# Fused attention and two dense blocks on one core: gate jobs spread through the second half, their stores on ScalarE's queue, and two moves in the attention phase

## The chip, the cores and the metric

The kernel runs on one core of one Trainium2 chip. The metric is the device time of one execution in microseconds (us). The engines go by the profile's names: PE (TensorE's matmuls) and PEld (its weight loads), DVE (VectorE), ACT (ScalarE), POOL (GpSimd) and SP (SyncE, which here only issues DMAs).

## The reference

Three blocks follow each other, on 4 batches of 448 rows and 768 columns (12 heads of 64).

```
attn = sigmoid(q @ k.T / sqrt(64) - log(448)) @ v        # per batch and head
x    = attn, heads side by side                           # 4 x 448 x 768

h    = (x.T @ U @ V).T                                    # mixes the rows, rank 32
u    = x + h
y    = u + relu(u @ w_ch1) @ w_ch2                        # 768 -> 3072 -> 768

gate = sigmoid(sum over k of conv_w[k] * y[row - 4 + k])  # 5 taps along the rows
out  = (gate * (y @ w_val)) @ w_out
```

## The kernel before, in words

**Products.** Every matmul operand is kept as a high and a low half, and `mm3` multiplies three times: high by high, high by low, low by high. The third of the three is thus the first to read the low half of its weights:

```
mm(ps, wk[:, 0], x[:, 0], start=start, stop=False, **kw)    # L438
mm(ps, wk[:, 0], x[:, 1], start=False, stop=False, **kw)    # L439
mm(ps, wk[:, 1], x[:, 0], start=False, stop=stop, **kw)     # L440
```

The high half is a copy on ACT (`in_two`, L200), the low half a subtraction on DVE (L203) that `in_two` puts into the list `deferred`; `flush()` writes that list out at the next part of a product.

**Three phases.** The attention phase has 12 rounds of two (batch, head pair)s: `scores` (L523), sigmoid (L511), `values` (L554), and `scores_rest`, `attend_rest` (L567) for the last columns of both pairs, after which `attend_rest` copies both results to `xs` (L576). Between these stand slots `(round, 0)`, `(round, 1)`, `(round, 2)`, in which `between()` runs what the table `side` holds: units that mix the rows of a finished batch (`mix_units`; `add` multiplies `h` at L758 and adds it to `xs` at L761), and preparations of weights.

The main phase computes y for two halves of the batches, first batches 0 and 1, then 2 and 3. A half has six quads q of four row blocks of the hidden layer. A quad has two chains, c = 0 and c = 2, of seven products each (`seven`), and then `ch2` four times, which multiplies the four relu'd blocks h by w_ch2 and adds the result to `xs` (L939). In a chain the products are `x` (A11), `y` (A12), `x` (S2), `z` (S1), `x` (S3), `z` (S4 with B22), and `x` (A22), which runs inside the next chain or ch2. The weights' combinations A and S are the work of DVE and ACT. Three copies on ACT (L807) save sums that the next product would write on: `p1`, `u2`, `p5`. `p5` copies z after S1; the part S4 writes z again, so its first matmul waits for that copy.

The last phase computes the gate of batches 2 and 3, the products with w_val and w_out, and the output.

**What decides the order of the side work.** `plan()` fills the list `jobs` in an order written by hand, and `step()`, which a product calls at its end, takes one job of it by `pump()`, at a few steps two. In the second half a quad has the jobs of the four row blocks' weights (`pair_jobs`, `second_jobs`), the preparation of w_val and w_out (`form_jobs`, the list `more`, for five of the six quads), and three jobs for one gate of batches 0 and 1 (`gate_jobs`): `first` (a scaled copy on ACT, L993, and one add on DVE, L989), `second` (two adds) and `third` (one add, then the sigmoid on ACT, L1005, then the store of 448 KB, L1010, on SP's queue). An add reads and writes 128 x 896 values. At the ends of the first three quads, `u_sums` also forms and parks sums T of y on DVE and ACT.

**Queues.** Every engine works its instructions in order, SP's DMA issues too. Loads of w_ch1's and w_ch2's prepared parts (L159, L417), of raw w_val (L163) and stores of prepared parts (L332) share SP's queue.

Of the kernel before, what the change touches and what calls it, by code (L numbers as in the profile page):

```python
# [30 lines left out]
NP = B * H // 2  # L31
# [16 lines left out]
def tile_kernel(  # L48
# [18 lines left out]
    nc = tc.nc  # L67
    mm = nc.tensor.matmul
    f32 = lambda ap: ap.bitcast(F32)
    deferred = []  # L70
# [4 lines left out]
    def flush(every=False):  # L75

        while deferred:
            now, deferred[:] = deferred[:], []
            for part in now:
                part()  # L80
            if not every:
                return
# [65 lines left out]
    gates_kept = {}  # L148
# [383 lines left out]
    def scores_rest(q):  # L532

        ps = pools["ps_s"].tile([P, 2, 512], F32, tag="sc", name=f"sl{q}")
        for j in range(2):
            kq, _ = raws.pop(2 * q + j)
            for h in range(2):
                r = slice(D * h, D * h + D)
                mm(
                    ps[D * j:D * j + D, h, :S],  # L540
                    kq[r, 0, NKC * SC + USED:],
                    kq[r, 1],
                    start=True,
                    stop=True,
                )
        rests[q] = rests[q], sigmoid(f"al{q}", ps)
# [15 lines left out]
    def attend_rest(q):  # L562
        vl, a = rests.pop(q)
        for j in range(2):
            r = slice(D * j, D * j + D)
            for h in range(2):
                mm(  # L567
                    pairs[2 * q + j][2]["ps"][D * h:D * h + D, :S],
                    vl[r, h],
                    a[r, h],  # L570
                    start=False,
                    stop=True,
                )
        for j in range(2):
            b, m = divmod(2 * q + j, KC)
            nc.vector.tensor_copy(x_of(b, m), pairs.pop(2 * q + j)[2]["ps"][:, :S])  # L576
# [404 lines left out]
    def gate_jobs(bs, m):  # L981

        t = []
        r = slice(bs[0], bs[-1] + 1)
        y = lambda k: xs[:, m, r, k:k + S]
        tap = lambda k: f32(cw[:, m * TAPS + k:m * TAPS + k + 1])

        def add(k):
            nc.vector.scalar_tensor_tensor(t[0], y(k), tap(k), t[0], op0=ALU.mult, op1=ALU.add)  # L989

        def first():
            t.append(operand(f"g{bs[0]}_{m}", F32)[:, :, :])
            nc.scalar.activation(t[0], y(0), AF.Copy, scale=tap(0))  # L993
            deferred.append(lambda: add(1))

        def second():
            add(2)
            add(3)

        def third():  # L1000
            add(4)
            deferred.append(sigmoid)

        def sigmoid():
            nc.scalar.activation(t[0], t[0], AF.Sigmoid)  # L1005
            deferred.append(put)

        def put():
            gates_kept[m] = pools["gates"].tile([P, 2, S], F32, tag="gates", name=f"gk{m}")
            nc.sync.dma_start(gates_kept[m][:, :, :], t[0])  # L1010

        return [(0, first), (0, second), (0, third)]

# [17 lines left out]
    def attention_phase():  # L1031


        for p, kq in enumerate([load_kq(p) for p in range(2)]):
            load_v(p, kq)
        nc.vector.memset(bias, -math.log(S))
        warm = scratch("warm")[:, :1]
        nc.scalar.activation(warm, bias, AF.Sigmoid)
        nc.gpsimd.memset(xs[:, :, :, :PAD], 0.0)

        zeros = operand("zeros")
        nc.vector.memset(f32(zeros[:, 0]), 0.0)
        idle = pools["ps_s"].tile([P, 2, 512], F32, tag="sc", name="idle")
        for _ in range(IDLE):
            mm(idle[:, 0, :S], zeros[:, 0, :P], zeros[:, 0], start=True, stop=True)
        prep_pair(0)
        load_pair(2)
        consts = load_mix()
        steps = prep_mix(*consts)
        side = {(0, 2): steps[:1], (1, 1): steps[1:2], (1, 2): steps[2:]}  # L1050
        for b in halves[0]:
            units = mix_units(b)
            r = 3 * b + 3
            for at, some in (
                ((r, 2), units[:2]),
                ((r + 1, 0), units[2:4]),
                ((r + 1, 2), units[4:5]),
                ((r + 2, 0), units[5:6]),
                ((r + 3, 0) if b == 0 else (r + 2, 2), units[6:]),
            ):  # L1060
                side[at] = some
        rounds = NP // 2
        todo = [part for k in range(KH) for part in u_sums(0, k)]
        def put(at, *parts):
            side[at] = side.get(at, []) + list(parts)

        put((0, 2), *[lambda: load_next(nc.sync)] * RAWS)
        at = iter([(q, k) for q in range(1, rounds) for k in range(3)][2:])
        for key in full_keys + part_keys:
            for part in ahead[key]:  # L1070
                slot = next(at)
                side[slot] = [part] + side.get(slot, [])
        for slot, n in (((9, 0), 1), ((9, 1), 1), ((9, 2), 2), ((10, 0), 1), ((10, 1), 1), ((10, 2), 2), ((11, 0), 1)):
            put(slot, *todo[:n])
            del todo[:n]
        for slot, n in (((10, 1), 1), ((10, 2), 1), ((11, 0), 1), ((11, 1), 2), ((11, 2), 2)):
            put(slot, *[pump] * n)

        def values(p):
            for c in range(NKC):  # L1080
                attend(p, c)

        def between(q, k):
            for step in side.get((q, k), ()):
                step()

        for q in range(rounds):
            p = 2 * q
            for c in range(NKC):
                scores(p, c)  # L1090
            flush()
            last = q == rounds - 1
            if q:
                values(p - 1)
                if last:
                    attend_rest(q - 1)
                between(q, 0)
                if not last:
                    attend_rest(q - 1)
            else:  # L1100
                prep_pair(1)
            if not last:
                scores_rest(q)
            flush()
            load_pair(p + 3)
            load_pair(p + 4)
            between(q, 1)
            prep_pair(p + 2)
            for c in range(NKC):
                scores(p + 1, c)  # L1110
            flush()
            values(p)
            between(q, 2)
            prep_pair(p + 3)
        scores_rest(rounds - 1)
        flush()
        pump()
        flush()
        values(NP - 1)
        attend_rest(rounds - 1)  # L1120

    full_keys = [("w2", n, half) for half in range(2) for n in range(QUAD)]
    part_keys = [("w2", n, 0) for n in range(QUAD, 2 * QUAD)]
# [2 lines left out]
    def plan():  # L1126

        for key in full_keys + part_keys:
            ahead[key] = ahead_jobs(*key, key in full_keys)
        def give(items):  # L1130
            for n, job, key in items:
                if key:
                    loads.append(key)
                jobs.append((n, job))

        rest = []
        for q in range(NQ):
            c1, c2 = (pair_jobs(0, QUAD * q + c) for c in (0, 2))
            w = second_jobs(0, q) if q else ready_jobs(0)
            w0, w1 = w[:len(w) - QUAD], w[len(w) - QUAD:]  # L1140
            raw, made = c2[:2] + c2[3:5], c2[2:3] + c2[5:]
            if not q:
                c1 = c1[:2] + c1[3:5] + c1[2:3] + c1[5:]
            a = c1[:4] + rest[:1] + c1[4:6] + rest[1:] + c1[6:7]
            for x in zip(raw, c1[7:] + [None]):
                a += x
            give(x for x in a if x)
            w01 = w0 + w1[:2]
            b = []
            for i in range(max(len(made), len(w01))):  # L1150
                b += made[i:i + 1] + w01[i:i + 1]
            if not q:
                b = made + w01
            give(b)
            rest = w1[2:]
        give(rest)
        more = [job for kind in ("val", "out") for k in range(KH) for job in form_jobs(kind, k)]
        share = -(-len(more) // (NQ - 1))
        for q in range(NQ):
            give(pair_jobs(1, QUAD * q))  # L1160
            a = pair_jobs(1, QUAD * q + 2) + (second_jobs(1, q) if q else ready_jobs(1))
            rest = [(*job, None) for job in gate_jobs(halves[0], q)] + more[:share]
            n = len(a)
            for i, job in enumerate(a):
                give([job] + rest[i * len(rest) // n:(i + 1) * len(rest) // n])
            del more[:share]
# [288 lines left out]
```

## Time and profile before

| | |
|---|---|
| three runs | 1014.51, 1015.64, 1016.39 us; median 1015.64 |
| the profiled execution | 1018.02 us; its span 1016.2 us |
| PE busy | 995.3 us (98%) |
| PEld busy | 843.1 us (83%) |
| DVE busy | 734.3 us (72%) |
| ACT busy | 464.3 us (46%) |
| mean granted TensorE clock | 0.993 of full speed |

The span reaches from the first instruction to the last; what the execution took beyond it, 1.8 us, lies around it. Times in rows count from the span's start. The attention phase lasts until about 150 us, the second half of the main phase from about 475 to 835 us.

### The profile page before, as it was taken

Reading aid. Unit: us, or ns where it says so; the run is one execution under the profiler, and the core shown is the slowest. Engines: PE = TensorE matmul, PEld = TensorE weight load, DVE = VectorE, ACT = ScalarE, POOL = GpSimd, SP = SyncE. Lnnn points to the kernel's source line nnn. Section 1 sums busy time; section 2 is a strip of 40 time slices with the busy share of each in tenths; the row PEclk is TensorE's granted clock in tenths of the full one; section 3 lists DMA queues with packets and bytes.
Section 4 is the critical chain, followed back from the end, with each engine's and each line's share of the span. In section 5 each row is a group of like instructions: output and inputs, shape, how many; then the busy total and the mean of one; then the engine's idle time right before and its main releaser. Section 6 shows DMA issues by size and latency. Waiting matters only on the chain.

```text
span 1016.2 us, 14576 instructions
## 1 busy us (share of the span) xinstructions
PE 995.3 (98%) x5208; PEld 843.1 (83%) x5208; DVE 734.3 (72%) x1324; ACT 464.3 (46%) x871; POOL 21.1 (2%) x39
## 2 busy tenths in 40 slices
PE   9999999999999999999989899998999999999998
PEld 5554448988888999999978798997999999999997
DVE  4767797658587888889466888878787667993631
ACT  6766685344352545546243453535353433431321
POOL 0111110000000000000000000000000000000000
PEclk9999999999999999999999999999999999999999
DMA  7967656625366686767274573735545186833845
GB/s 187 270 190 203 162 147 187 193 80 163 96 161 188 189 251 188 220 204 266 105 236 156 197 251 137 244 117 205 181 136 190 55 319 199 283 125 114 258 144 185
DMA packets 83048, 187.51 MB, mean 185 GB/s; under 512 B 15008, under 2 KB 34704, under 8 KB 82976
## 3 DMA queue, kind: packets, MB, share of 16 engines
q1 hardware_dynamic: 79840, 174.64, 55.0%
q0 software_dynamic: 2832, 11.60, 3.9%
q8 instruction: 41, 0.67, 0.3%
q10 hardware_dynamic: 304, 0.34, 0.1%
q14 instruction: 31, 0.25, 0.1%
HBM read 129.14 MB, written 57.41 MB: 184 GB/s over the span
## 4 chain that ended last, share of the span: by engine, by line
PE 91%; DVE 5%; DMA 2%; ACT 1%; issue 1%; SPq 0%; DVEq 0%; ACTq 0%
PE ch L438 11%; PE ch L439 11%; PE ch L440 11%; PE x L438 5%; PE x L440 5%; PE x L439 5%; PE av L554 5%; PE sc L523 5%; PE z L438 3%; PE z L440 3%; PE z L439 3%; PE x_fin L438 1%; PE x_fin L440 1%; PE val L439 1%; PE val L438 1%; PE x_fin L439 1%
## 5 line engine op out<-in xcount | busy, mean ns | idle before, releaser
L438 PE MATMUL ch<-h,w 128*128 128x448 f32 x576 | 212.8, 369 | 4.0 <-DMA w<-s_w 4.0
L439 PE MATMUL ch<-h,w 128*128 128x448 f32 x576 | 211.6, 367 | 0.0
L440 PE MATMUL ch<-h,w 128*128 128x448 f32 x576 | 211.5, 367 | 0.0
L939 DVE TENSOR_TENSOR xs<-ch,xs 128x1344 f32<-128x1344 f32 x48 | 74.6, 1555 | 68.0 <-PE ch L440 67.7
L438 PEld LDWEIGHTS ch<-h,w 128*128 128x128 f32 x576 | 108.5, 188 | 16.3 <-issue 4.3
L440 PEld LDWEIGHTS ch<-h,w 128*128 128x128 f32 x576 | 108.5, 188 | 9.7
L439 PEld LDWEIGHTS ch<-h,w 128*128 128x128 f32 x576 | 108.6, 189 | 9.5
L511 ACT ACTIVATE a<-sc,bias 128x896 f32<-128x896 f32 x72 | 67.6, 1010 | 11.0 <-PE sc L523 10.8
L104 DVE SCALAR_TENSOR_TENSOR x_w<-x_w,r_w 128x384 uint32<-128x384 uint32 x84 | 46.9, 559 | 29.8 <-ACT x_w L100 23.6
L554 PE MATMUL av<-a,vr 128*64 128x448 f32 x288 | 59.4, 548 | 0.0
L523 PEld LDWEIGHTS sc<-ks 64*128 64x128 f32 x432 | 38.8, 190 | 22.6 <-issue 6.6
L523 PE MATMUL sc<-ks 64*128 64x448 f32 x432 | 53.9, 389 | 1.9 <-DVE ks L500 0.8
L100 ACT ACTIVATE x_w<-raw_w 128x384 f32<-128x384 f32 x84 | 45.6, 546 | 19.9 <-DMA raw_w<-in_w 6.3
L440 PE MATMUL x<-T,S 128*128 128x448 f32 x144 | 52.9, 367 | 0.0
L438 PE MATMUL x<-T,S 128*128 128x448 f32 x144 | 52.8, 366 | 0.0
L439 PE MATMUL x<-T,S 128*128 128x448 f32 x144 | 52.7, 366 | 0.0
L554 PEld LDWEIGHTS av<-a,vr 128*64 128x64 f32 x288 | 18.5, 136 | 30.0 <-issue 26.7
L200 ACT ACTIVATE S<-raw_x_w 128x384 fp32r<-128x384 f32 x48 | 23.0, 517 | 37.2 <-PE ch L440 17.6
L200 ACT ACTIVATE A<-x_w 128x384 fp32r<-128x384 f32 x36 | 18.5, 522 | 46.3 <-PE ch L440 40.8
L200 ACT ACTIVATE A<-raw_x_w 128x384 fp32r<-128x384 f32 x36 | 18.2, 519 | 40.4 <-PE ch L440 37.1
L438 PE MATMUL z<-B,S 128*128 128x448 f32 x72 | 27.5, 382 | 7.8 <-ACT p L807 7.8
L807 ACT ACTIVATE p<-x 128x448 f32<-128x448 f32 x24 | 13.1, 545 | 47.7 <-PE x L440 45.0
(303 smaller groups left out, 2188.3 us busy)
## 6 DMA issues: line engine op xcount, KB each, us to landing
raw_w<-in_w SPq DMA_DIRECT2D x79, 384.0 KB, 3.8
kq<-in_kq SPq DMA_DIRECT2D x46, 224.0 KB, 4.4
raw_x_w<-k_w SPq DMA_DIRECT2D x24, 384.0 KB, 3.6
k_w<-x_w SPq DMA_DIRECT2D x43, 192.0 KB, 4.0
f_val_A<-s_val_A SPq DMA_DIRECT2D x21, 384.0 KB, 3.8
f_out_S<-s_out_S SPq DMA_DIRECT2D x20, 384.0 KB, 3.5
k_h<-x_w SPq DMA_DIRECT2D x36, 192.0 KB, 3.7
raw_w<-in_w POOLq DMA_DIRECT2D x17, 384.0 KB, 4.5
```

The costliest lines, as they stand in the source:

```text
L100: nc.scalar.activation(f32(x), f32(high), AF.Prelu, scale=2.0 ** -112, alpha=-(2.0 ** 32))
L104: nc.vector.scalar_tensor_tensor(x, x, 3, r, op0=ALU.logical_shift_left, op1=ALU.bitwise_or)
L200: nc.scalar.activation(t[:, 0], x, AF.Copy)
L438: mm(ps, wk[:, 0], x[:, 0], start=start, stop=False, **kw)
L439: mm(ps, wk[:, 0], x[:, 1], start=False, stop=False, **kw)
L440: mm(ps, wk[:, 1], x[:, 0], start=False, stop=stop, **kw)
L511: nc.scalar.activation(a[:, :, :], ps[:, :, :S], AF.Sigmoid, bias=bias, scale=1.0 / math.sqrt(D))
L523: mm(ps[:, h, :S].rearrange("p (c s) -> p c s", c=NSC), ks[r, tk, 0, c], ks[r, tq, 1, :, :SC], start=t == 0, stop=t == 2,)
L554: mm(att["ps"][D * h:D * h + D, :S], vr[:, h, c], a[:, h], start=c == 0, stop=False,)
L807: nc.scalar.activation(t, ps, AF.Copy)
L939: nc.vector.tensor_add(y, three[:, :, :S], y)
```

## The change

Four things are edited.

- A finished gate is stored by ACT's DMA queue right behind the sigmoid, in the same step; before, `put` was deferred and issued by SP.
- `plan()` puts the three gate jobs among the form jobs of the quad (at one sixth, one half and five sixths of them) and no longer ahead of them. In the last quad there are no form jobs and nothing changes.
- In the attention phase the last mix unit of batch 1 goes from slot (8, 2) to (9, 0), one place later. Batch 0's stood one place later already.
- In the last round, `scores_rest` comes ahead of the jobs of slot (11, 2), and `values` and `attend_rest` come ahead of the last `pump()`.

```
         def sigmoid():
             nc.scalar.activation(t[0], t[0], AF.Sigmoid)
-            deferred.append(put)
-
-        def put():
             gates_kept[m] = pools["gates"].tile([P, 2, S], F32, tag="gates", name=f"gk{m}")
-            nc.sync.dma_start(gates_kept[m][:, :, :], t[0])
+            nc.scalar.dma_start(gates_kept[m][:, :, :], t[0])
...
-                ((r + 3, 0) if b == 0 else (r + 2, 2), units[6:]),
+                ((r + 3, 0), units[6:]),
...
             values(p)
+            if last:
+                scores_rest(q)
             between(q, 2)
             prep_pair(p + 3)
-        scores_rest(rounds - 1)
-        flush()
+        values(NP - 1)
+        attend_rest(rounds - 1)
         pump()
         flush()
-        values(NP - 1)
-        attend_rest(rounds - 1)
...
-            rest = [(*job, None) for job in gate_jobs(halves[0], q)] + more[:share]
+            rest = more[:share]
+            for i, job in enumerate(gate_jobs(halves[0], q)):
+                rest.insert((2 * i + 1) * len(more[:share]) // 6 + i, (*job, None))
```

**Place 1: the first chain of the second quad.** Names are tiles: `g_1` is the gate of column block 1, `p_1_4`, `x_4` and `z_4` belong to the chain of row blocks 4 and 5 in the second half, `T_y` are the sums that are parked. DVE before, around the three last adds of the gate:

```order
L989 SCALAR_TENSOR_TENSOR g_1_5796<-xs,cw,g_1_5796 128x896
L584 TENSOR_TENSOR T_y_5799<-T_T_y_5738,T_y_5799 128x448
L584 TENSOR_TENSOR T_y_5801<-T_T_y_5738,T_y_5801 128x448
L864 TENSOR_TENSOR p_1_4_5794<-p_1_4_5794,y_4_5798 128x448
L251 TENSOR_TENSOR raw_x_w_7_1_5742<-raw_x_w_7_1_5742 128x384
L252 TENSOR_TENSOR raw_x_w_6_1_5673<-raw_x_w_7_1_5742,raw_x_w_6_1_5673 128x384
L989 SCALAR_TENSOR_TENSOR g_1_5796<-xs,cw,g_1_5796 128x896 x3
L859 SCALAR_TENSOR_TENSOR h_2_5836<-p_1_4_5794,h_2_5836 128x448
L256 TENSOR_TENSOR raw_x_w_6_1_5673<-raw_x_w_6_1_5673 128x384
L864 TENSOR_TENSOR p_1_4_5848<-p_1_4_5848,x_4_5774 128x448
```

The same stretch of DVE now:

```order
L584 TENSOR_TENSOR T_y_5797<-T_T_y_5738,T_y_5797 128x448
L584 TENSOR_TENSOR T_y_5799<-T_T_y_5738,T_y_5799 128x448
L864 TENSOR_TENSOR p_1_4_5794<-p_1_4_5794,y_4_5796 128x448
L203 TENSOR_TENSOR A_val_5810<-x_val_0_5652,A_val_5810 128x384
L203 TENSOR_TENSOR A_val_5812<-x_val_1_5668,A_val_5812 128x384
L251 TENSOR_TENSOR raw_x_w_7_1_5742<-raw_x_w_7_1_5742 128x384
L252 TENSOR_TENSOR raw_x_w_6_1_5673<-raw_x_w_7_1_5742,raw_x_w_6_1_5673 128x384
L101 TENSOR_SCALAR r_val_0_5841<-raw_val_0_5745 128x384
L104 SCALAR_TENSOR_TENSOR x_val_0_5840<-x_val_0_5840,r_val_0_5841 128x384
L859 SCALAR_TENSOR_TENSOR h_2_5847<-p_1_4_5794,h_2_5847 128x448
L989 SCALAR_TENSOR_TENSOR g_1_5860<-xs,cw,g_1_5860 128x896
L864 TENSOR_TENSOR p_1_4_5858<-p_1_4_5858,x_4_5774 128x448
```

Of the four adds one is left in this chain. On ACT the copy `p5` of z_4 (which is written to `p_1_4_5848`, and now to `p_1_4_5858`) stood behind the gate's sigmoid:

```order
L807 ACTIVATE u_1_4_5833<-x_4_5774 128x448
L858 ACTIVATE h_2_5836<-p_1_4_5794 128x448
L1005 ACTIVATE g_1_5796<-g_1_5796 128x896
L807 ACTIVATE p_1_4_5848<-z_4_5775 128x448
L200 ACTIVATE A_val_5864<-x_val_0_5652 128x384
```

It now stands behind a relu, with the gate's first copy behind it:

```order
L807 ACTIVATE u_1_4_5838<-x_4_5774 128x448
L100 ACTIVATE x_val_0_5840<-raw_val_0_5745 128x384
L858 ACTIVATE h_2_5847<-p_1_4_5794 128x448
L807 ACTIVATE p_1_4_5858<-z_4_5775 128x448
L993 ACTIVATE g_1_5860<-xs,cw 128x896
```

The sigmoid and the store behind it stand some thirty instructions later, among the splits that run beside ch2.

**Place 2: the end of the second chain of the same quad, ahead of ch2.** `w_1_4_0` is the first block of w_ch2 that ch2 reads, and its low half is the L203 row. DVE before:

```order
L203 TENSOR_TENSOR A_1_6_5973<-raw_x_w_7_1_5742,A_1_6_5973 128x384
L859 SCALAR_TENSOR_TENSOR h_2_5975<-p_1_6_5911,h_2_5975 128x448
L353 TENSOR_TENSOR x_val_1_5668<-x_val_1_5668,x_val_0_5652 128x384
L864 TENSOR_TENSOR p_1_6_5989<-p_1_6_5989,x_6_5894 128x448
L203 TENSOR_TENSOR w_1_4_0_6003<-raw_x_h__2_1_5918,w_1_4_0_6003 128x384
L203 TENSOR_TENSOR w_1_5_0_6004<-raw_x_h__2_1_5918,w_1_5_0_6004 128x384
```

And now:

```order
L353 TENSOR_TENSOR x_val_1_5668<-x_val_1_5668,x_val_0_5652 128x384
L989 SCALAR_TENSOR_TENSOR g_1_5860<-xs,cw,g_1_5860 128x896 x2
L859 SCALAR_TENSOR_TENSOR h_2_5967<-p_1_6_5913,h_2_5967 128x448
L203 TENSOR_TENSOR A_1_6_5984<-raw_x_w_7_1_5742,A_1_6_5984 128x384
L864 TENSOR_TENSOR p_1_6_5982<-p_1_6_5982,x_6_5897 128x448
L203 TENSOR_TENSOR S_val_5999<-x_val_0_5652,S_val_5999 128x384
L203 TENSOR_TENSOR S_val_6001<-x_val_0_5840,S_val_6001 128x384
L357 TENSOR_TENSOR x_val_0_5840<-x_val_1_5886,x_val_0_5652 128x384
L864 TENSOR_TENSOR u_1_6_5965<-u_1_6_5965,z_6_5898 128x448
L203 TENSOR_TENSOR w_1_4_0_6019<-raw_x_h__2_1_5891,w_1_4_0_6019 128x384
L203 TENSOR_TENSOR w_1_5_0_6020<-raw_x_h__2_1_5891,w_1_5_0_6020 128x384
```

The two adds of the gate are new in this chain. The two low halves of `S_val`, the sum L357 and the sum `u` with `z_6` stood behind the low half of `w_1_4_0` and now stand ahead of it. In the next three quads the two adds stand in the same chain too, a few rows ahead of the low half of the block that ch2 reads first, but `u` stays behind it.

**Place 3: SP's queue in the first quad of the second half.** `w_1_0_0` is again the first block that ch2 reads, here a load of a part prepared long before. Before:

```order
L1010 DMA gk_5345<-g_0_5285 128x896
L163 DMA raw_val_1_5364<-in_wval 128x384
L163 DMA raw_val_0_5391<-in_wval 128x384
L163 DMA raw_val_1_5409<-in_wval 128x384
L163 DMA raw_val_0_5417<-in_wval 128x384
L332 DMA s_val_A_5434<-A_val_5428 128x768
L332 DMA s_val_A_5437<-A_val_5430 128x768
L417 DMA w_1_0_0_5450<-s_w_0_0_446 128x768
```

And now:

```order
L332 DMA s_val_A_5377<-A_val_5367 128x768
L332 DMA s_val_A_5380<-A_val_5369 128x768
L163 DMA raw_val_1_5402<-in_wval 128x384
L163 DMA raw_val_0_5420<-in_wval 128x384
L163 DMA raw_val_1_5428<-in_wval 128x384
L159 DMA raw_x_w_4_1_5444<-k_w_2138 128x768
L417 DMA w_1_0_0_5458<-s_w_0_0_446 128x768
```

The two stores went from just ahead of the load to further up, a load of a part of w_ch1 (L159) came in just ahead of it, and the gate's store has left the queue.

## Rows read from the trace of the kernel before

**Rows 1.** The page: busy time by engine, and the chain that ended last.

```profile
PE 995.3 (98%) x5208; PEld 843.1 (83%) x5208; DVE 734.3 (72%) x1324; ACT 464.3 (46%) x871; POOL 21.1 (2%) x39
...
PE 91%; DVE 5%; DMA 2%; ACT 1%; issue 1%; SPq 0%; DVEq 0%; ACTq 0%
```

**Rows 2.** Waits of PE over the span: waiter, releaser, total us, times, longest.

```profile
PE z L438 <- ACT p L807: 7.8, 3, 3.1
PE ch L438 <- DMA w<-s_w: 4.0, 2, 3.0
...
PE y L438 <- DVE xs L576: 1.0, 1, 1.0
...
PE sc L523 <- DVE xs L761: 0.7, 1, 0.7
```

**Rows 3.** Timeline, PE, second quad: start, duration, line, tiles, [idle before, releaser].

```profile
568.96 0.36 PE L440 MATMUL x<-T,S 128*128 128x448 f32 x1
572.40 0.47 PE L438 MATMUL z<-B,S 128*128 128x448 f32 x1 [3.08 <-ACT p L807]
...
573.35 0.58 PE L439 MATMUL z<-B,S 128*128 128x448 f32 x1
573.72 0.58 PE L440 MATMUL z<-B,S 128*128 128x448 f32 x1
```

**Rows 4.** Timeline, DVE, the same stretch.

```profile
567.41 3.52 DVE L989 SCALAR_TENSOR_TENSOR g<-xs,cw,g 128x896 f32<-128x896 f32 x3
```

**Rows 5.** Timeline, ACT, the same stretch.

```profile
570.97 0.95 ACT L1005 ACTIVATE g<-g 128x896 f32<-128x896 f32 x1 [3.92 <-DVE g L989]
571.83 0.53 ACT L807 ACTIVATE p<-z 128x448 f32<-128x448 f32 x1
```

**Rows 6.** Busy us by engine in six stretches; last three: granted clock, DMA share, GB/s.

```profile
525.00:530.00 5.00, 4.01 (x13) 3.65 (x14) 0.00 (x0) 0.00 (x0) 0.00 (x0) 0.66 0.99 340
570.00:575.00 5.00, 2.60 (x9) 2.35 (x10) 4.29 (x8) 3.94 (x8) 0.00 (x0) 0.83 0.38 147
575.00:580.00 5.00, 5.00 (x23) 4.57 (x22) 3.00 (x8) 1.35 (x3) 0.00 (x0) 0.83 0.56 184
630.00:635.00 5.00, 4.13 (x13) 3.71 (x14) 3.35 (x8) 3.54 (x8) 0.00 (x0) 0.66 0.48 170
690.00:695.00 5.00, 3.72 (x13) 3.34 (x14) 3.67 (x8) 3.46 (x7) 0.00 (x0) 0.78 0.23 92
700.00:800.00 100.00, 100.00 (x486) 90.83 (x485) 74.64 (x130) 42.80 (x89) 0.00 (x0) 1.00 0.49 164
```

**Rows 7.** Timeline, SP's DMA issues, first quad of the second half.

```profile
519.93 0.80 SPq L332 DMA_DIRECT2D s_val_A<-A_val  x2
520.77 0.53 SPq L417 DMA_DIRECT2D w<-s_w  x1
```

**Rows 8.** Timeline, PE, the start of that quad's ch2.

```profile
522.59 0.37 PE L440 MATMUL z<-B,S 128*128 128x448 f32 x1
525.99 0.71 PE L438 MATMUL ch<-h,w 128*128 128x448 f32 x1 [3.03 <-DMA w<-s_w]
```

**Rows 9.** Timeline, DVE, second quad, the end of its second chain.

```profile
587.12 0.62 DVE L864 TENSOR_TENSOR p<-p,x 128x448 f32<-128x448 f32 x1 [0.86 <-ACT S_val L200]
587.65 1.02 DVE L203 TENSOR_TENSOR w<-raw_x_h__2_1_5918,w 128x384 fp32r<-128x384 f32 x2
```

**Rows 10.** Timeline, PE, second quad: the third matmul of its ch2.

```profile
589.08 0.36 PE L440 MATMUL ch<-h,w 128*128 128x448 f32 x1
```

**Rows 11.** Line L989, the gate's adds: count, duration in ns, first and last start.

```profile
L989 DVE SCALAR_TENSOR_TENSOR g<-xs,cw,g x24: 1142/1147/1153, 502.6 to 821.9; 128x896 f32<-128x896 f32 x24
```

**Rows 12.** Timeline, DVE, the end of the attention phase.

```profile
152.11 0.35 DVE L101 TENSOR_SCALAR r_w<-raw_w 128x384 uint32<-128x384 uint32 x1
...
153.04 1.15 DVE L576 COPY xs<-av 128x448 f32<-128x448 f32 x2
...
155.12 1.02 DVE L203 TENSOR_TENSOR S<-x_w,S 128x384 fp32r<-128x384 f32 x2
```

## The prediction

> **What bounds the kernel now.** I read the page first, for the engine that leaves no room: PE is busy 98% of the span and makes up 91% of the chain that ended last, DVE 5%, DMA 2%, ACT 1% [rows 1]. So time is gained where PE stands still, or where its clock is low, and nowhere else; a DVE instruction or a DMA more costs nothing until PE waits for it. Second come PE's waits, which list those places. The reader is to see four of interest [rows 2]: `z` waits 7.8 us in three places for the ACT copy L807, ch2 waits 4.0 us in two places for loads of w_ch2, `y` waits 1.0 us for the copies L576, and `sc` 0.7 us for the mix unit's add L761.
>
> Third, the timeline of one `z` wait tells whose delay it is. DVE works on three gate adds from 567.41 for 3.52 us [rows 4]. The gate's sigmoid on ACT waits 3.92 us for them and runs at 570.97, and behind it in ACT's order, at 571.83, comes the copy p5 that the next product needs [rows 5]. PE, done with its matmuls at 568.96, goes on at 572.40 [rows 3].
>
> Fourth, the granted clock by stretch. It reads 0.66 to 0.83 of full speed in the stretches that follow stalls of this size, and 1.00 from 700 to 800 us, where PE does not wait [rows 6]. Two stretches of 5 us at 0.83 lack 1.7 us of full clock, as one at 0.66 does. That fits 3.4 us at the lower of the two levels, 1.2 instead of 2.4 GHz. In such a time a matmul starts every 0.37 us (573.35 and 573.72) [rows 3], against 0.206 us at the full clock (486 matmuls in the 100 us from 700 on [rows 6]). 3.4 us hold 9.2 matmuls, which take 1.9 us at 0.206. So each drop costs about 1.5 us. Four such drops follow stalls: one after ch2's wait at 522.6 and three after the `z` waits. The waits of about 1 us (ch2's other one of 4.0 less 3.0, and that of `y` [rows 2]) show none; I take a stall over 2 us as the condition, which is an estimate from these cases.
>
> **The change part by part.** The sum is made against the profiled execution, 1018.02 us; the median of the runs is 1015.64, so I carry the difference over to the median.
>
> *Gates spread, first chain.* Of the four gate adds that stood in a quad's first chain or the jobs around it, one stays there in the second quad, behind the copy's inputs; the sigmoid goes to ch2, where ACT has splits but no p5 to do. The copy p5 then follows a relu, and z ended long before. So all three `z` waits should go: 7.8 us [rows 2] and three drops of 1.5 us, 12.3 us. If adds of the second chain delayed its p5 in the same way, a part would come back; on ACT nothing that waits for a gate now stands ahead of a p5, so I take all of it. Bound from below: only two of three go, 8.2 us.
>
> *SP's queue in the first quad.* The two stores that stood just ahead of the load w_1_0_0 were issued at 519.93 and the load at 520.77 [rows 7], and the load landed for 525.99, 3.03 us late [rows 8]. The stores now go earlier, since their splits do, and the gate's store has left the queue. In front of the load stands a load of w_ch1, whose buffer comes free with a split on ACT; from the rows around, I put the issue at about 519.1, 1.7 us earlier. The 16 DMA engines are busy in that stretch, with a share of 0.99 [rows 6], and the transfers that move out of the stretch (the gate's store was done earlier anyway) relieve it by one to two of 384 KB; at 340 GB/s one takes 1.2 us. So the load arrives 1.7 to 4 us sooner, against 3.03 wanted. I take a stall of 0.3 left. Then the drop behind it goes too: 2.7 + 1.5 = 4.2 us. Bounds: 0 and 4.5. The second load wait, 1.0 us, is behind stores that also go earlier: 0.8 (0 to 1).
>
> *The adds' new place.* Second and third add are one job, 2 x 1.15 us [rows 11], and it now stands in the second chain. Before, the low half of w_1_4_0 began at 587.65 and took about 0.55, half of the row's 1.02 for two [rows 9]; its first reader, the third matmul of ch2, ran at 589.08 [rows 10]: 0.9 us to spare, and DVE had idled 0.86 shortly before [rows 9]. Now 2.3 us of adds, and some 1.5 us of low halves and a sum (three at about 0.5), stand ahead of it: 3.8 - 0.9 - 0.86 = 2.0 us late at most by this difference. Walked through in the new order, from the sum with x_4 on, 27 instructions at their spacings give 15.5 us and one wait for a relu 1.3; the low half is then 1.6 us late. And since the sum `u` now stands ahead of it and waits for the last matmul of z_6, it is late by about 0.9 even with an empty DVE. I take 1.6 for the second quad (0.9 to 2.0, with a drop 3.5). The same walk gives 0.55, 0 and 0.6 in the three quads after it, where `u` is not ahead and DVE has no more to do than before the adds: 2.7 in all, with 0.9 and 8 as ends. The first quad's low halves are loaded, so nothing there, and the last quad is unchanged.
>
> *The stores on ACT.* Six DMA issues come to ACT, in ch2 stretches where ACT is busy two fifths of the time (42.80 of 100 us [rows 6]) and PE reads nothing that is fresh from it. At the 0.5 us of an issue on SP (0.53 [rows 7]), six are 3 us in 100s of idle ones: 0. If ch2's splits waited for them, 3.
>
> *The two moves in attention.* The add L761 goes behind another product, and `sc` no longer waits for it: 0.7 (0 to 0.7). The copies L576 at 153.04 stood behind the unpacking that the last `pump()` gave DVE (from 152.11 on [rows 12]); they now run 0.9 earlier and `y` starts 0.9 earlier. But the next part needs the low half of S, whose row is at 155.12 [rows 12] and stays there, with the unpacking now behind the copies. So most is given back one product later: 0.25 (0.2 to 0.9).
>
> Sum: -12.3 - 4.2 - 0.8 + 2.7 + 0 - 0.7 - 0.25 = -15.55. 1018.02 becomes 1002.5, and the median 1015.64 becomes **1000.1; I say 1000**.
>
> **The rivals.** *The loads land no earlier.* What speaks for it: a DMA share of 0.99 when the load is under way [rows 6], so bytes, and not the issue, may set the landing. Then 4.2 and 0.8 stay: -10.55, 1005. Against it: the stores ahead of it are 768 KB, and they go earlier by more than their own transfer takes. The Trainium skill, "DMA: Bandwidth & Descriptors", section "Issuing engines are not separate DMA queues", says that DMAs started by different engines run on the same 16 DMA engines and interleave, so that another issuing engine saves issue time only; by that rule the gate's store leaves SP's queue without relief to the others, which is this rival's case. My sum rests on the times of issue, not on the store's new queue.
>
> *The adds' new place costs more.* The low half is late by over 2 us in two of the four quads and the clock falls each time: 2 x (2.0 + 1.5) + 1.2 = 8.2 instead of 2.7, -10, 1005.6; in all four 14, -4.3, 1011. For it: DVE is the second busiest engine (72% [rows 1]), and the adds stand right before the edge. Against it: the walk.
>
> *The z waits don't go.* The change then fails of its main effect: another split ahead of p5 on ACT waits for a DVE that is as late as before. All three waits and drops stay: -3.25, 1012.4; against it, ACT's order shows no instruction of a gate ahead of p5 but the first scaled copy.
>
> *Slower.* A store on ACT waits until the gate's new buffer or one of the DMA's own semaphores is free, and what is queued behind it is the splits of w_ch2's next blocks and the p1 copy of the next quad, for which PE waits. A DMA here can take 5 us from its issue (the load of 520.77 [rows 7] let PE go on at 525.99 [rows 8]). With ACT's slack of some 2 us there, 5 us of holding in each of five quads make 15, and a drop of 1.5 each 7.5 more: -15.55 + 22.5 = +7, 1022.6. It decides from a hold of about 4 us a quad: a stall of 2 us and the drop are 3.5, where 3.1 in each of five quads cancel the gain. For it: ACT's rows behind the store are in order, and nothing overtakes. Against it: five of the six stores wait for their own sigmoid alone. The Trainium skill, "TensorE: Matmul & The Clock Gate", section on the array's architectural detail, calls ACT's queue strict first in, first out; p5 behind the sigmoid [rows 5] agrees.
>
> **How the numbers follow.** Forecast 0.62 (its own range 996.5 to 1003.5: all new waits at their low ends give 998, with the whole load wait and y's 0.9 gone 997; the high ends short of a drop give 1003). Loads no earlier 0.13; dearer adds 0.15; z waits stay 0.04; slower 0.03; no change by these cancelling 0.03. Range: 995.5 to 1006.5, which takes in the first two rivals. A difference under 0.2% (2 us) is what a measurement of this kernel can't tell from no change. Faster 0.93, same 0.03, slower 0.04.
>
> **What would show it.** Right: no wait of `z` for L807; the clock at 1.00 from 500 to 700 but for at most one drop; the first ch2 wait below 1 us; new waits of `ch` L440 for DVE L203, longest in the second quad at 1 to 2 us; no `sc` wait for L761; `y` earlier, and a new wait for a low half of S behind it. Wrong: a wait of ACT behind L1007, a `ch` wait over 2 us with a clock below 0.9 behind it, or a load wait that stays near 3 us.

## The result, and the profile after

The changed kernel takes 1004.32 us (median of 4 runs, 999.46 to 1007.91) against 1015.08 us (median of 4 runs, 1013.48 to 1016.39). The ratio is 0.989, with a 95% interval of 0.985 to 0.994: faster by about 1.1%. The forecast was 1000 us, with a range of 995.5 to 1006.5. The profiled execution took 1007.91 us, span 1006.1 us, so it is the slowest of the four. In the experiments below, two executions (1957.70 us, of the changed kernel run again, and 1957.56 us, the one that was profiled of the late adds with the store on SP, whose waits are thus not known) took nearly twice the time of all others at a clock of 1.00 and are left out of medians and ratios.

The page of the changed kernel, busy time and chain, as in [rows 1]:

```profile
PE 991.0 (99%) x5208; PEld 839.7 (83%) x5208; DVE 733.9 (73%) x1324; ACT 465.0 (46%) x871; POOL 21.0 (2%) x39
...
PE 74%; DVE 6%; DMA 3%; ACT 2%; issue 1%; SPq 0%; DVEq 0%; ACTq 0%
```

PE is as before the engine that is always busy, with 4 us less busy time for the same 5208 matmuls. A busy microsecond at the low clock does about half the work (a matmul every 0.37 us [rows 3]), and three drops of 3.4 us instead of four make 1.7 us of it; most of the rest goes with the two paces that the last section tells of. PE's waits, to be read against [rows 2]:

```profile
PE ch L440 <- DVE w L203: 4.7, 4, 2.9
PE idle L1042 <- DVE zeros L1039: 1.4, 1, 1.4
PE sc L523 <- DVE ks L500: 1.3, 1, 1.3
...
PE x L440 <- DVE S L203: 0.8, 2, 0.5
PE ch L438 <- DMA w<-s_w: 0.7, 1, 0.7
PE ch L438 <- ACT w L200: 0.4, 1, 0.4
```

Times are totals, counts and longest waits, as in [rows 2]. The three `z` waits are gone. The load waits fell from 4.0 to 0.7 us, and the waits of `y` for L576 and of `sc` for L761 went. In their place ch2's third matmul waits 4.7 us for w_ch2's low half, in the second to fifth quads, and smaller waits have come. Busy time and clock by stretch (the last three numbers: granted clock, DMA share, GB/s) show where the clock falls now:

```profile
5.00:10.00 5.00, 3.50 (x22) 2.28 (x26) 3.48 (x9) 2.00 (x3) 0.00 (x0) 0.81 0.79 185
10.00:15.00 5.00, 5.00 (x34) 2.26 (x32) 2.10 (x5) 4.20 (x5) 0.00 (x0) 0.85 0.80 191
...
525.00:530.00 5.00, 5.00 (x26) 4.53 (x25) 4.01 (x9) 2.14 (x5) 0.00 (x0) 1.00 0.47 183
580.00:585.00 5.00, 2.14 (x10) 1.65 (x10) 4.96 (x11) 2.40 (x5) 0.00 (x0) 0.99 0.71 240
585.00:590.00 5.00, 5.00 (x18) 4.47 (x17) 2.21 (x5) 1.43 (x4) 0.00 (x0) 0.67 0.84 310
750.00:755.00 5.00, 3.47 (x16) 2.55 (x16) 4.89 (x10) 2.64 (x5) 0.00 (x0) 1.00 0.60 191
755.00:760.00 5.00, 5.00 (x19) 4.52 (x18) 4.08 (x9) 1.78 (x4) 0.00 (x0) 0.66 0.57 164
```

The four drops of before [rows 6] are gone, also the one behind the first load wait (525 to 530 us at 1.00). Two new ones stand behind new waits, at 585 and 755 us, and one in the first 15 us, which the change does not touch.

The largest new wait is in the second quad. First the timeline of DVE there, with one row of the fifth quad:

```profile
568.90 0.36 DVE L101 TENSOR_SCALAR r_val<-raw_val 128x384 uint32<-128x384 uint32 x1 [2.05 <-DMA raw_val<-in_wval]
...
577.02 2.33 DVE L989 SCALAR_TENSOR_TENSOR g<-xs,cw,g 128x896 f32<-128x896 f32 x2
...
582.33 0.61 DVE L864 TENSOR_TENSOR u<-u,z 128x448 f32<-128x448 f32 x1
582.86 1.02 DVE L203 TENSOR_TENSOR w<-raw_x_h__2_1_5891,w 128x384 fp32r<-128x384 f32 x2
...
741.32 0.36 DVE L101 TENSOR_SCALAR r_out<-raw_out 128x384 uint32<-128x384 uint32 x1 [2.05 <-DMA raw_out<-in_wout]
```

And that of PE, the third matmul of the second quad's ch2:

```profile
583.47 0.47 PE L440 MATMUL ch<-h,w 128*128 128x448 f32 x1 [2.86 <-DVE w L203]
```

Where [rows 9] had the low half done 0.9 us ahead of its reader [rows 10], the reader now waits 2.86 us. The two adds stand ahead of it, as the order said. But DVE had also stood idle for 2.05 us earlier in the quad, waiting for a load of raw w_val, and had not caught up; the last row is the like in the fifth quad, for raw w_out. That idle time was not in the prediction's walk, though DVE waited for the load in this place before the change too:

```profile
578.93 0.36 DVE L101 TENSOR_SCALAR r_val<-raw_val 128x384 uint32<-128x384 uint32 x1 [1.32 <-DMA raw_val<-in_wval]
```

### The profile page after: what moved, and what is told of

It is laid out like the page before. It is cut to its first block, busy times and chain, and to the rows that moved or that the text cites. A ratio compares the mean times of both kernels' runs of the same rounds, so it can differ in the third digit from the quotient of the medians.

```text
span 1006.1 us, 14552 instructions
## 1 busy us (share of the span) xinstructions
PE 991.0 (99%) x5208; PEld 839.7 (83%) x5208; DVE 733.9 (73%) x1324; ACT 465.0 (46%) x871; POOL 21.0 (2%) x39
## 4 chain that ended last, share of the span: by engine, by line
PE 74%; DVE 6%; DMA 3%; ACT 2%; issue 1%; SPq 0%; DVEq 0%; ACTq 0%
PE ch L440 12%; PE ch L438 12%; PE ch L439 12%; PE x L440 4%; PE x L438 4%; PE x L439 4%; PE z L439 2%; PE z L440 2%; PE z L438 2%; PE x_fin L440 1%; PE val L440 1%; PE val L438 1%; PE x_fin L438 1%; PE x_fin L439 1%; PE val L439 1%; PE y L439 1%
## 5 line engine op out<-in xcount | busy, mean ns | idle before, releaser
L440 PE MATMUL ch<-h,w 128*128 128x448 f32 x576 | 211.8, 368 | 4.7 <-DVE w L203 4.7
L440 PEld LDWEIGHTS ch<-h,w 128*128 128x128 f32 x576 | 108.3, 188 | 15.7 <-DVE w L203 6.2
L440 PE MATMUL x<-T,S 128*128 128x448 f32 x144 | 53.2, 369 | 0.8 <-DVE S L203 0.8
L200 ACT ACTIVATE S<-raw_x_w 128x384 fp32r<-128x384 f32 x48 | 23.1, 518 | 37.6 <-DVE raw_x_w L252 21.6
L200 ACT ACTIVATE A<-x_w 128x384 fp32r<-128x384 f32 x36 | 18.5, 522 | 46.4 <-PE ch L440 40.7
L200 ACT ACTIVATE A<-raw_x_w 128x384 fp32r<-128x384 f32 x36 | 18.2, 519 | 38.9 <-PE ch L440 38.2
L858 ACT ACTIVATE h<-p 128x448 fp32r<-128x448 f32 x48 | 27.5, 573 | 16.5 <-DVE p L864 16.3
L807 ACT ACTIVATE p<-x 128x448 f32<-128x448 f32 x24 | 13.0, 544 | 43.9 <-PE x L440 41.2
```

The source lines that it names most:

```text
L200: nc.scalar.activation(t[:, 0], x, AF.Copy)
L807: nc.scalar.activation(t, ps, AF.Copy)
L858: nc.scalar.activation(t[:, 0], x, AF.Relu)
```

## The experiments

Two questions were open: which of the four parts brings the gain, and what makes the low half late: the place of the adds, or the loads. Each ratio is the kernel's time to that of the kernel before in the same series, with its 95% interval.

**The changed kernel again.**

> The changed kernel once more. If the waits that the profile of the changed kernel shows are its own and not those of one execution, the ratio to before is 0.989 again (0.985 to 0.993), z does not wait for L807, and ch L440 waits for DVE L203 in the second to fifth quads, with the longest wait at 2.5 to 3 us in the second quad. If the two clock drops behind these waits and the stretches in which a matmul starts every 0.207 instead of 0.203 us come and go between executions, the sums of the waits agree but the span differs by up to 4 us.

Ratio 0.991 (0.988 to 0.994); its five runs go from 1002.29 to 1007.79 us. No `z` wait; ch L440 waits four times for L203, 3.5 us, the longest 1.4 us in the second quad and not 2.5 to 3. Behind none of them the clock falls. Its raw w_val load in the second quad landed 3.7 us after its issue (5.4 us in the profile above) and let DVE go on without an idle gap. So the wait's place belongs to the kernel, and its size to the execution.

**Parts alone.** The spread of the gate jobs alone:

```
-            rest = [(*job, None) for job in gate_jobs(halves[0], q)] + more[:share]
+            rest = more[:share]
+            for i, job in enumerate(gate_jobs(halves[0], q)):
+                rest.insert((2 * i + 1) * len(more[:share]) // 6 + i, (*job, None))
```

> Only the gate jobs spread; the store stays deferred on SP's queue, the attention phase as before. Theory (the spread alone brings the gain): about 1005 us, ratio 0.990 (0.985 to 0.995); no z wait for L807, the load wait of the first quad at 1 us or less. Rival (the store's new queue frees SP for the loads): the z waits go, but ch2's waits for loads stay near 4 us with a clock drop, about 1009 us, ratio 0.994.

Ratio 0.990 (0.987 to 0.993), the whole gain. No `z` wait, the load wait at 0.8 us in the profile with the store on SP. The rival falls. One drop of the clock is left in its profile, in the fifth quad.

The store on ACT alone:

```
-            deferred.append(put)
-
-        def put():
             gates_kept[m] = ...
-            nc.sync.dma_start(gates_kept[m][:, :, :], t[0])
+            nc.scalar.dma_start(gates_kept[m][:, :, :], t[0])
```

> Only the store on ACT's queue; the gate jobs stand ahead of the form jobs as before. Theory: z waits 7.8 us in three places as before and ch2 about 4 us for loads, ratio 1.000 (0.997 to 1.003). Rival (SP's queue relieved): ch2's wait for loads falls to 1 us and a drop of the clock goes, about 4.5 us, ratio 0.9955.

Ratio 1.0033 (1.0013 to 1.0054): slower. Both expectations missed. PE's waits, and ACT's timeline at the second quad's `z` wait (compare [rows 2] and [rows 5]):

```profile
PE z L438 <- ACT p L807: 9.4, 3, 3.6
PE ch L438 <- DMA w<-s_w: 4.7, 2, 4.0
```

```profile
571.70 0.95 ACT L1005 ACTIVATE g<-g 128x896 f32<-128x896 f32 x1 [3.92 <-DVE g L989]
572.68 0.33 ACTq L1007 DMA_DIRECT2D gk<-g  x1
573.05 0.54 ACT L807 ACTIVATE p<-z 128x448 f32<-128x448 f32 x1 [0.40 <-ACT g L1005]
```

With the gate jobs at their old place, the store's issue stands between sigmoid and p5. ACT is idle for 0.40 us over it, and the three `z` waits grow by 1.6 us together. The first load wait was longer too (4.0 us), though the load was issued at 520.77 as in [rows 7]: SP's queue was not what held it. In this profile two of the four drops also last about twice as long as before (the clock reads 0.50 from 525 to 530 us, where [rows 6] has 0.66), so how much of the 0.3% is the stall at p5 itself is not parted.

The two moves in attention alone (the third and fourth part of the diff):

> Only the two moves in the attention phase. Theory: sc no longer waits 0.7 us for L761, y no longer 1.0 us for L576, but the part x with S waits 0.5 to 0.8 for the low half L203 instead; in all 0.3 to 0.7 us, ratio 0.9995, not to be told from 1. Rival (the earlier copies carry through): 1.7 us, ratio 0.998.

Ratio 0.998 (0.996 to 1.001), not told from 1; the runs go from 1009.96 to 1018.86 us. In the profile the waits for L761 and L576 are gone; 0.5 us of `x` for the low half of S has come. (`sc` waits 1.5 us for L500 instead of 0.8, but that is at 6.7 us of the span, where the program has only begun and none of the moved instructions has run.)

The changed kernel with the store back on SP:

> The changed kernel with the gate's store back on SP's queue, deferred: the spread and the two moves in attention. Theory (the store's new queue is worth nothing once the sigmoid stands beside ch2): 1003 to 1005 us, the time of the changed kernel within 0.3%, ratio to before 0.988 to 0.991. Rival (each store costs ACT some 0.4 us that PE feels at ch2 too): 2 us faster than the changed kernel, ratio 0.987. Second rival (SP's queue needs the relief): the ch2 load wait of the first quad returns to 3 us, ratio 0.995.

Ratio 0.990 (0.987 to 0.994), a median of 1004.67 us: once the sigmoid stands beside ch2, the store's queue makes no difference that was measured. Its load waits are 0.5 us, so SP did not need the relief.

**The cost of the adds' place.** Without the second job's adds (the gate's two middle taps are left out):

```
         def second():
-            add(2)
-            add(3)
+            pass
```

> The changed kernel without the gate's second job, so the two middle taps of the gate of batches 0 and 1 are left out; it shows what the place of these adds costs. Theory (they are what makes w_ch2's low half late): the ch L440 waits for L203 fall from 3.5 to 4.7 us to under 1 us, no clock drop stands behind them, about 1000 us, ratio 0.985 to 0.987. Rival (DVE is late there because it waits about 2 us for raw w_val and w_out): the waits of the second and fifth quads stay above 1 us and the time moves by under 2 us.

Ratio 0.986 (0.982 to 0.989), 999.05 us. The row that was 4.7 and 3.5 us:

```profile
PE ch L440 <- DVE w L203: 1.4, 2, 1.0
```

Two waits are left, in the second and third quads, and the clock reads 1.00 throughout. The theory holds in the main; the 1.0 us of the second quad is what the order alone costs, with the sum `u` ahead of the low half. But DVE's own waits for the raw loads were short in this trace (0.68 us in the second quad, 0.56 us in the fifth), so this run alone does not part the adds from the loads.

The adds beside ch2, by moving the second and third job to the end of the quad's list:

```
-                rest.insert((2 * i + 1) * len(more[:share]) // 6 + i, (*job, None))
+                rest.insert(len(rest) if i else len(more[:share]) // 6, (*job, None))
```

> The changed kernel with the gate's second and third job at the end of the quad's jobs, beside ch2, with nothing left out. Theory: as without the adds, 1000 us, ratio 0.985; only the second quad may keep about 0.9 us, where the sum u with z_6 stands ahead of the low half. Rival (three adds in a row, 3.5 us, hold up ch2's own add L939 or another low half): a new wait of ch for DVE of over 1 us in most quads, 1004 to 1006 us.

Ratio 0.998 (0.996 to 1.001): nearly all of the gain is lost, and by neither of the two ways. PE's waits, then DVE and PE in the third quad:

```profile
PE ch L438 <- DMA w<-s_w: 4.4, 2, 3.6
PE ch L440 <- DVE w L203: 4.3, 2, 3.5
PE x L438 <- ACT u L807: 2.5, 1, 2.5
```

```profile
641.42 0.36 DVE L101 TENSOR_SCALAR r_out<-raw_out 128x384 uint32<-128x384 uint32 x1 [2.97 <-DMA raw_out<-in_wout]
```

```profile
643.55 0.47 PE L440 MATMUL ch<-h,w 128*128 128x448 f32 x1 [3.53 <-DVE w L203]
```

The low half is late again with no add ahead of it. Taking the second gate job out of the middle of the list moves the form jobs behind it one step forward, so that they ask for raw w_out before it has landed; DVE waits 2.97 us for it, with w_ch2's low half queued behind. (In the changed kernel this unpacking runs at 642.00 us, behind that low half at 640.83.) The rival of the run before (the raw loads) is thus a cause of its own. The 2.5 us of `x` have it too: the copy `u2` on ACT (L807, fifth quad) stands behind an unpacking that waits 4.0 us for raw w_out. What held the load of the 3.6 us was not followed.

The same with the store on SP:

> As the kernel with the late adds, with the gate's store deferred on SP's queue. Theory: the same time within 0.2%. Rival (a store on ACT costs there): 1 to 2 us faster.

Ratio 0.998 (0.996 to 1.001), the same.

So the list should stay as it is, and only the adds move between the gate's own jobs. All three in the third job, then the same with the store on SP, then one add moved and one left (the comments say what differs there):

```
         def second():
-            add(2)
-            add(3)
+            pass              # one add moved: add(2)
         def third():
+            add(2)            # one add moved: without this line
+            add(3)
             add(4)
```

> The changed kernel with the job list as it is, but the gate's second and third add done in its third job, beside ch2, instead of the second; nothing is left out. Theory (their place ahead of ch2 is the cost, and beside ch2 DVE has room): as without the adds, 999 to 1000 us, ratio 0.985 to 0.987, ch L440 waits for L203 at 1 to 1.5 us, no clock drop from 500 to 800. Rival (three adds of 1.15 us in a row hold up w_ch2's other low halves or ch2's add L939, as in the kernel with the late adds): new ch waits for DVE of 1 us or more in several quads, 1003 us or more.

> The same with the gate's store deferred on SP's queue. Theory: the same time within 0.2%, since the store stands beside ch2 in either queue. Rival: the store on ACT delays the splits of w_ch2 behind it by 0.4 us a quad, so this one is 1 to 2 us faster.

> The changed kernel with one of the two adds moved from the gate's second to its third job. Theory: half of the effect, ch L440 waits for L203 at 2 to 2.5 us, no stall over 2 us and so at most one clock drop, 1001 to 1003 us. Rival (threshold rather than sum, a low half is late only by what exceeds DVE's slack): as without the adds, 999 to 1000 us.

Ratios 0.986 (0.985 to 0.988), 0.984 (0.982 to 0.986) and 0.984 (0.982 to 0.986). With all three in the third job, L440's waits are 1.4 us in either kernel, as without the adds, and no others of 1 us stand in several quads. The trace with the store on ACT also parts the two causes. In the second quad DVE waits 2.86 us for the raw w_val load, longer than the 2.05 us of the changed kernel, and PE waits no longer than without the adds:

```profile
570.52 0.36 DVE L101 TENSOR_SCALAR r_val<-raw_val 128x384 uint32<-128x384 uint32 x1 [2.86 <-DMA raw_val<-in_wval]
583.24 0.48 PE L440 MATMUL ch<-h,w 128*128 128x448 f32 x1 [1.01 <-DVE w L203]
```

In the fifth quad DVE waits 2.00 us for raw w_out, and PE not at all for the low half. With the list in this order a late load alone does no harm; the low half is late where the adds stand behind the load as well. With one moved, the wait is that of the theory and the time (1000.16 us) that of the rival:

```profile
PE ch L440 <- DVE w L203: 2.0, 2, 1.6
```

Last, one add moved, with the store on SP:

> The two parts that helped together: the gate jobs spread with one add moved from the second to the third job, and the store deferred on SP's queue, with the moves in attention. Theory (the store beside ch2 costs ACT 0.3 us an issue and PE nothing): 1000 us, ratio 0.982 to 0.986, as with the store on ACT. Rival (the store on ACT costs some 2 us at ch2, as between the two kernels with three adds in the third job): 998 us, ratio 0.982 or less.

Ratio 0.987 (0.984 to 0.990) and 1004.05 us, slower than both expectations, so the 2 us between the two kernels with three adds do not come again with this pair, and the store's queue stays without a measured effect. The four kernels with moved adds have medians of 1000.06 to 1004.05 us. Over all their 19 runs the mean is 1001.3 us, and over the 21 runs of the three kernels with the spread and the adds at the changed kernel's place (the changed kernel in both series) it is 1004.6: 3.4 us apart, with twice the standard error at 1.5. The runs are from several chips, so this difference is a weaker statement than the ratios. By both measures they beat the kernel before and the changed one; which of the four is best is not settled.

## Why the prediction was right, and where not

The median, 1004.32 us, lies in the stated range, which was made to take in two of the rivals; the forecast's own range, 996.5 to 1003.5 us, it misses by 0.8 us. Of the signs of being wrong one came in the profiled execution (a `ch` wait of 2.86 us with the clock at 0.67 behind it), and not in the second one.

**What bounds the kernel** and **gates spread**: right. All 7.8 us of `z` waits went and none came back, and with them three drops of the clock. The spread alone gives 0.990.

**SP's queue in the first quad**: right, and nearly with the right size. The load was issued at 519.06 (519.1 was worked out), behind the w_ch1 load as the order said, and PE went on with 0.67 us of wait (0.3 was forecast) instead of 3.03. Of these 2.36 us the load's earlier landing gives 1.9 (524.11 instead of 525.99); the rest is that PE came to it 0.5 us later. SP's issues, then PE:

```profile
518.68 0.33 SPq L159 DMA_DIRECT2D raw_x_w<-k_w  x1
519.06 0.42 SPq L417 DMA_DIRECT2D w<-s_w  x1
```

```profile
524.11 0.44 PE L438 MATMUL ch<-h,w 128*128 128x448 f32 x1 [0.67 <-DMA w<-s_w]
```

The drop behind it went too, and so did the second load wait. The rival that loads land no earlier is out. What helped is the spread, for the two kernels with it, the adds at this place and the store on SP have it as well (0.8 and 0.5 us); that it does so by way of the earlier stores is what the order says, and was not tried by itself.

**The adds' new place**: the right mechanism, the wrong size. This is the term that failed. It was put at 2.7 us (0.9 to 8). The waits of ch for L203 are 4.7 us, and two drops of the clock of about 1.5 us each make it 7.7. In the other execution it is 3.5 without a drop, quad by quad 1.4, 0.6, 0.5 and 1.0 against the walk's 1.6, 0.55, 0 and 0.6. The walk held DVE's own work to be all that delays the low half. In the trace DVE waits for a raw load in the second quad (2.05 us) and for another in the fifth (2.05 us). In the second it goes with the time the load takes: 5.4 us from issue to landing here, 3.7 us in the execution without the gap, 4.3 us before the change. In the fifth it is 1.9 to 2.1 us in every trace with the spread and all four adds, against 0.55 us before, so there it belongs to the kernel rather than to one execution (only where two of the adds are left out is it 0.56 us, and why it is short there stays open). The rival "the adds' new place costs more" (two of four quads with a drop, 1005.6 us) is what the profiled execution shows, and the median lies between it and the forecast.

**A stall over 2 us as the condition for a drop**: fell. In the changed kernel's fifth quad (timeline of PE) ch2 waits 0.39 us and then 1.14 us, and the clock falls from 755 us on. In the kernel with the spread alone it falls in the same place behind 0.66 and 0.88 us (0.66 from 750 to 755 us). The two rows of either:

```profile
752.81 0.47 PE L438 MATMUL ch<-h,w 128*128 128x448 f32 x1 [0.39 <-ACT w L200]
...
754.63 0.47 PE L440 MATMUL ch<-h,w 128*128 128x448 f32 x1 [1.14 <-DVE w L203]
```

```profile
749.38 0.47 PE L438 MATMUL ch<-h,w 128*128 128x448 f32 x1 [0.66 <-ACT w L200]
...
750.93 0.60 PE L440 MATMUL ch<-h,w 128*128 128x448 f32 x1 [0.88 <-DVE w L203]
```

In the kernel with the spread alone the longest of these waits, 1.7 us in the second quad, brings none:

```profile
PE ch L440 <- DVE w L203: 3.4, 4, 1.7
```

The size of a single stall does not decide it. (A single load wait of 1.93 us, in the kernel with three adds in the third job and the store on SP, brought one: 0.69 from 525 to 530 us.) Nor is the price fixed: the four drops of [rows 6] cost about 1.5 us each, but in the profile of the two moves in attention alone three of four last about twice as long (0.50 from 575 to 580 us).

**The stores on ACT**: costless in the changed kernel, as predicted, but only because of the spread: at the old place they cost 0.3%. The slower rival's mechanism, ACT's strict order, is thus real, with 0.4 us a store in place of the 4 us or so it needed. (PE does read what is fresh from ACT at ch2, against what the prediction held: it waits 0.4 us there for a high half, L200. With the spread alone, where SP stores, it waits 0.7 us.)

**The two moves in attention**: 0.95 us was the sum. The waits went as predicted, and the `x` part gave back 0.5 us for the low half of S. Its row, 155.48 and not 155.12 [rows 12], looks later than the prediction held, but everything there is: the changed kernel's `sc` waited 1.3 instead of 0.8 us for L500 at the very start, which the moves do not touch. So PE's rows are to be compared with their neighbours, first before, then now:

```profile
106.64 0.98 PE L567 MATMUL av<-al,vl 64*64 64x448 f32 x8
118.85 0.98 PE L567 MATMUL av<-al,vl 64*64 64x448 f32 x8
...
149.71 0.98 PE L567 MATMUL av<-al,vl 64*64 64x448 f32 x8 [0.29 <-ACT al L511]
156.05 0.36 PE L440 MATMUL x<-T,S 128*128 128x448 f32 x1
```

```profile
107.23 0.98 PE L567 MATMUL av<-al,vl 64*64 64x448 f32 x8
118.66 0.98 PE L567 MATMUL av<-al,vl 64*64 64x448 f32 x8
...
150.04 0.98 PE L567 MATMUL av<-al,vl 64*64 64x448 f32 x8 [0.28 <-ACT al L511]
156.08 0.47 PE L440 MATMUL x<-T,S 128*128 128x448 f32 x1 [0.47 <-DVE S L203]
```

PE was 0.59 us later ahead of the moves, 0.19 us earlier behind the first of them, 0.33 us later at the end of the phase and 0.03 us later in the part with S. So the first move gave 0.78 us at its place (0.7 was forecast), and the rounds behind it took 0.52 us of that back; the end of the phase gave 0.30 us (0.25 was forecast), with the low half of S no later than its neighbours. The prediction had no term for the 0.52. Together 0.56 us are left, which no timing here can tell from nothing.

**The sum.** For the profiled executions: 13.5 us of the waits in [rows 2] became 7.1 (4.7, 0.8, 0.7 and 0.4, and 0.5 more of `sc` for L500), 6.4 us saved. Four drops in the main phase became two, 3 us. That makes 9.4 us; the span fell by 10.1. The 0.5 us of `sc` at the start is the execution's and not the change's. The drop in the first 15 us costs next to nothing: by 107 us PE is 0.59 us late, and the wait for L500 explains nearly all of it. What is left fits the two paces of the last section: from 475 us on, 1851 matmuls before and 1344 now started at the slower one, and 507 times 4 ns are 2.0 us. With the 0.5 us that attention gave back, 1.2 us are to be explained, so the account closes to about 1 us. The forecast had 15.55, and 5 of the 6 us between are the adds' place.

## What to carry to other kernels

A job that stands at the head of a list may be what paces the jobs behind it: taken away, it frees its own engine, but the others then ask for their loads earlier and may wait for them. When side work is moved, follow every job of the list to the transfer that it needs and to the first reader of what stands behind it. Splitting work between jobs that already stand in the list (moving an add from the second to the third) is safer than moving a job, and a DMA issue belongs on an in-order engine only where nothing urgent stands behind it.

## What was not expected of the hardware

At a granted clock of 1.00, PE runs this program at one of two paces. Busy time by stretch, of before:

```profile
900.00:950.00 50.00, 50.00 (x244) 45.41 (x243) 30.33 (x54) 13.11 (x26) 0.00 (x0) 1.00 0.43 136
```

And of the changed kernel:

```profile
590.00:640.00 50.00, 50.00 (x243) 45.41 (x243) 43.07 (x75) 24.29 (x50) 0.00 (x0) 1.00 0.54 182
...
900.00:950.00 50.00, 50.00 (x248) 46.35 (x247) 27.41 (x49) 13.14 (x26) 0.00 (x0) 1.00 0.55 172
```

In 50 us without a wait PE has 243 or 244 matmuls, or 248, of the same shape under way. In the traces that is 0.2067 or 0.2027 us from start to start (the counts take in matmuls that began just ahead of the stretch). The same part of the program (900 to 950 us) has the one pace in one execution and the other in the next. In the traces here the pace mostly changes at a wait and stays until a later one. Over the 360 us of the main phase's second half the difference is some 7 us, as much as the runs of one kernel differ (1002.29 to 1007.79 us). Whether this is what makes them differ was not tried, and what sets the pace stays open.
